# Softmax attention and a linear attention on one Trainium2 core: the end of the last unit rebuilt, and a build-time scheduler given new weights

## The chip, the cores and the metric

The kernel runs on one core of one Trainium2 chip. The metric is the time of one execution on the device in microseconds (us). The kernel before was run five times: 786.75, 781.05, 789.01, 781.58 and 782.21 us, so the median is 782.21 us.

The core has five engines that run side by side, each with its own list of instructions in a fixed order: TensorE (PE, matrix products into PSUM), VectorE (DVE), ScalarE (ACT, activation functions such as Exp), GpSimd (POOL), and SyncE (SP), which issues most DMA transfers. An instruction waits on semaphores for its inputs; all that stands behind it on its engine waits with it.

## The reference

Two independent blocks on sequences of 2048 rows of 512 numbers, 32 heads of 16, in bf16. Their outputs stand side by side in `out[2048, 1024]`.

```python
# A: full softmax attention
q, k, v = split(x @ wqkv)                        # [32, 2048, 16] each
p = softmax(q @ k.T * 16**-0.5)                  # [32, 2048, 2048]
a = merge(p @ v) @ wo
# B: linear attention with a learned feature map
phi = lambda t: concat(softmax(t @ w_phi), softmax(-(t @ w_phi)))   # 16 -> 32 features
kv, z = phi(k).T @ v, phi(k).sum(rows)
b = merge((phi(q) @ kv) / (phi(q) @ z + 1e-6)) @ wo
```

A makes 32 x 2048 x 2048 exponentials, and these are most of the kernel's work.

## The kernel before, in words

**Units and tiles.** A's work is cut into 32 units: a group of four heads (`g`, eight of them) for 512 queries (`c`, four of them). A unit has 16 key tiles of 128 keys. For one key tile and one head TensorE makes a score tile of 128 keys by 512 queries (L696, four heads in four row quarters of the array). The exponential comes in two ways:

- On ScalarE (L900): one Exp over two or three score tiles at once, straight out of PSUM into the ring `pT`. There are 645 Exps of two tiles and 86 of three, which makes 1,548 score tiles or 387 key tiles.
- On VectorE: 125 key tiles. A multiply-add (L957) writes an integer that, read as fp16, is a piecewise linear exponential; three more copies with an added phase (L978) go with scaled values `VJ`, so that four such curves add up to a good one. Five of a unit's 16 key tiles (`DK`) may go this way.

Then p @ v follows (L703, four column quarters of the array), which adds up in one PSUM bank per unit; a column of ones in V yields the row sums. When a unit is done, VectorE copies its bank to `X` (L750), SyncE sends the sums through DRAM so that their reciprocals come back spread over the partitions (`sums`, `scr`, `Yd`), and GpSimd multiplies (L782). After eight units the rows of a query block are projected (L1023), copied to `OA` and stored (L1039).

**B runs beside A.** Its steps are released when A has reached given shares of its key tiles (`b0`, `b1`, `b2`). The key half has 16 steps, and each has 32 small products of 34 columns (L1147).

**The order is planned when the kernel is built.** `_Sched` holds a queue per stream of tasks, each with an estimated duration and latency. It places next the task that can start earliest, moved by the stream's weight in `_W`, and so writes each engine's list. The chip follows that list with semaphores and no clock of its own. How many key tiles go to VectorE is no constant: it falls out of the planned times (`src_a`, `src_d`). `act_exp` plans an Exp of n tiles at 0.187 + 0.3657 n us.

**Fillers.** Before each TensorE task `_fill` looks at the planned activity of the array in the 3.42 us before (`_recent`). If TensorE would be idle anyway, it inserts products of zero (L730, four in a group) while the activity is under `ACTIVE` = 0.60; under `FORCE` = 0.40 it inserts one even where that delays the task. There are 448 of them, from 65 us on.

**The last unit** does without the way through DRAM (`last_unit`). One fp32 product (L799) spreads the row sums over the partitions into a bank of the pool `G`, which has four banks. VectorE takes four reciprocals of 128 columns each (L805), and after each one multiplies (L808). Meanwhile TensorE has added the other units' share of the four output row groups (L815), each in a `G` bank of its own; the last product of a group (L821) needs that part's multiply. Then three row groups are copied by ScalarE (L1031) and one by VectorE (L1035) into `OA`, which has two places, and stored by SyncE. Five range checks of the sums (L838) run on VectorE in between; they set a flag that leads to a slow general path when a sum is out of range.

Of the kernel before, what the change touches and what calls it, by code (L numbers as in the profile page):

```python
# [157 lines left out]
class _Sched:  # L158
# [5 lines left out]
    MM = 0.216  # L164
    PE_LAT = 0.21
    WINDOW = 3.42
    ACTIVE = 0.60
    FORCE = 0.40

    def __init__(self):  # L170
        self.free = {}
        self.busy = {}
        self.streams = {}
        self.end = 0.0
        self.mode = None
        self.rows = [0.0] * 4
        self.port = {"dve": 0.0, "pool": 0.0}
        self.urgent = None
        self.last_port = None
        self.filler = None  # L180
        self.ahead = lambda: 0
        self.active = collections.deque()
        self.nfill = 0
        self.nforce = 0
# [39 lines left out]
    def _choose(self, eng, ss):  # L224
        cand = []
        for s in ss:
            if not s["q"] and s["src"] is not None:
                s["src"](s)
            if s["q"]:
                t = s["q"][0]  # L230
                if t.prep is not None:
                    t.prep(t)
                r = self._ready(t) if t.gate is None or t.gate() else None
                if r is not None:
                    st = self._start(t, r)
                    w = s["w"]
                    cand.append([st, st + (w(t) if callable(w) else w) - _W["age"] * (st - r), s, r])
        if not cand:
            return None
        if eng == "pe" and self.urgent is not None:  # L240
            u = [c for c in cand if c[2] is self.urgent]
            if u:
                due = max(u[0][3], self.free["act"] + self.ahead() - self.MM - self.PE_LAT - _W["early"])
                for c in cand:
                    t = c[2]["q"][0]
                    if t.mode != "r" and c[0] + t.dur + self.SWITCH > due + 0.02:
                        c[1] += _W["guard"]
        c = min(cand, key=lambda c: c[1])
        return c[0], c[2]

    def run(self):
        while True:
            best = None
            for eng, ss in self.streams.items():
                c = self._choose(eng, ss)
                if c is not None and (best is None or c[0] < best[0]):
                    best = c
            if best is None:
                break
            self._place(best[1]["q"].popleft(), best[0])  # L260
        left = {e: [len(s["q"]) for s in ss] for e, ss in self.streams.items()}
        assert not any(any(v) for v in left.values()), left
# [10 lines left out]
    def _fill(self, t, start):  # L273


        e = max(self.free["pe"], max(self.rows))
        back = 0.0 if t.mode == "c" else self.SWITCH
        x = e if self.mode == "c" else e + self.SWITCH
        while True:
            a = self._recent(max(x, start - back))  # L280
            late = x + self.MM + back > start
            if a >= (self.FORCE if late else self.ACTIVE) or not self.filler(x):
                break
            self._record(x, x + self.MM, 1.0)
            x += self.MM
            self.nfill += 1
            self.nforce += late
            self.mode = "c"
            self.rows = [x] * 4
            self.free["pe"] = x  # L290
            if late:
                start = x + back
                break
        return start

    def _place(self, t, start):
# [41 lines left out]
        if t.then is not None:  # L338
            t.then(t)


_W = dict(tp=-0.226, qa=-0.02, qd_r=0.115, qd_o=0.235, pj=-0.051, pa_n=3, pa_w=0.053, pd_n=0, pd_w=0.105,
          b=-0.067, op=-0.004, dx=-0.238, dxe=-0.193, dev=-0.248, dop=-0.322, dn=-0.245, da=-0.165, dad=0.113,
          dek=-0.101, av=-0.057, kf=-0.03, v=0.039, kv=0.004, qf=-0.017, y=-0.203, t=0.061, o=0.176, df=-0.163,
          dred=-0.076, dv=-0.053, dkv=-0.118, dy=-0.02, dd=0.003, dob=-0.124, dmn=0.059, akf=-0.019,
          aqf=-0.072, aot=-0.365, age=0.03, early=0.0, guard=0.346, cut=5, lead=6, b0=0.286, b1=0.54, b2=0.99,
          p0=8, p1=30, p2=6.012, psh=0, pn=1, ps=-0.308, el=2, both=0, va=16, ka=8, ota=0, xlat=3.6)

_LOG2E = 1.4426950408889634
_NPH = 4  # L350
# [5 lines left out]
def _main_path(nc, es, P, dsem, flag, A_x, A_wqkv, A_wo, B_x, B_wqkv, B_w_phi, B_wo, out):  # L356
# [18 lines left out]
    SC = _Sched()  # L375
# [130 lines left out]
    def put(s, t):  # L506
        s["q"].append(t)
        return t
# [73 lines left out]
    def bank_of(f):  # L582
        return PS[:, f.res["b"].idx, :]
# [164 lines left out]
    def make_unit_end(u):  # L748
# [5 lines left out]
        def after_x(_):  # L754
            xi = xv.res["x"].idx
            d1 = put(sp_q, _Task("sp", 0.5, dma(d_s1[u % 2], lambda e, t, i: e.dma_start(
                sums[:, 16 * u:16 * u + 16], X[16 - g % 2:128:32, xi, :])), [xv], lat=2.2,
                rel=[lambda: [xv.res["x"]]]))
            if u == NU - 1:
                col.append(d1)  # L760
# [35 lines left out]
    def last_unit(xv, xi, c):  # L796


        bc = put(pe_op, _Task("pe", 0.9, pe_group(1, lambda e, t, i: e.matmul(  # L799
            PS[:, t.res["b"].idx, :], sel[:], X[:, xi, :], start=True, stop=True)), [xv], lat=PL, pre=[t_sel],  # L800
            need=[("b", G, 1, 4)]))
        parts = []
        for k in range(4):
            cs = slice(128 * k, 128 * k + 128)
            r = put(dv_n, _Task("dve", 0.98, one("dve", lambda e, t, cs=cs: e.reciprocal(  # L805
                Yd[:, parts[0][0].res["y"].idx if parts else t.res["y"].idx, cs], PS[:, bc.res["b"].idx, cs])), [bc], lat=DL,
                need=[] if parts else [("y", y_sl, 1, 4)], rel=[lambda: [bc.res["b"]]]))
            m = put(dv_n, _Task("dve", 0.22, one("dve", lambda e, t, cs=cs: e.tensor_tensor(  # L808
                Oo[:, parts[0][1].res["o"].idx if parts[0][1].res else t.res["o"].idx, cs], X[:, xi, cs],
                Yd[:, parts[0][0].res["y"].idx, cs], ALU.mult)), [r], lat=DL, need=[] if parts else [("o", oo_sl, 1, 1)],  # L810
                rel=[lambda: [parts[0][0].res["y"]]] + ([lambda: [xv.res["x"]]] if k < 2 else [])))
            parts.append((r, m))
        firsts = []
        for st in range(4):
            f = put(pe_op, _Task("pe", 4 * MM, pe_group(4, lambda e, t, p, st=st: e.matmul(  # L815
                bank_of(t), OT[:, c % 2, p, st * 128:(st + 1) * 128], WOp[:, p, :] if p < 3 else WOl[:, 0, :],
                start=(p == 0), stop=False)), [mul[8 * c + p] for p in (1, 3, 5, 6)] + [l_wo] + wol, need=[("b", G, 1, 1)]))
            firsts.append(f)
        for st in range(4):
            f = firsts[st]  # L820
            t = put(pe_op, _Task("pe", MM, pe_group(1, lambda e, t, i, st=st, f=f: e.matmul(  # L821
                bank_of(f), Oo[:, parts[0][1].res["o"].idx, st * 128:(st + 1) * 128], WOl[:, 1, :], start=False, stop=True)),
                [f, parts[st][1]], lat=PL))
            out_rows(c, st, f, t, st % 4 != 3)

    cnt = sb("cnt", [128, 8], F32)
    good = sb("good", [128, 1], BF)
# [65 lines left out]
    def act_exp(qk):  # L893

        pieces, b, n = qk.pieces, qk.first, len(qk.pieces)
        us = 0.187 + 0.3657 * n

        def ex_emit(e, t):
            p = slots(t)[0].idx
# [27 lines left out]
    def dve_kt(u, kt):  # L927
# [7 lines left out]

        def gate():

            if sum(x.left == 0 for x in G) > 1:
                return True
            return not any(s["q"] and s["q"][0].need and s["q"][0].need[0][1] is G  # L940
                           and all(d.done for d in s["q"][0].deps) for s in one_bank)
# [73 lines left out]
    pe_qd["src"] = src_d  # L1015

    d_oa = [dsem("oa0"), dsem("oa1")]
    op_done = {}

    def out_proj(c):  # L1020
        op_done[c] = []
        for st in range(4):
# [1 line left out]
                bank_of(t), OT[:, c % 2, p, st * 128:(st + 1) * 128], WOp[:, p, :], start=(p == 0), stop=(p == 3)),  # L1024
                [mul[8 * c + 2 * p + 1] for p in range(4)] + [l_wo], [("b", G, 1, 1)])
            op_done[c].append(t)
            out_rows(c, st, first, t, False)

    def out_rows(c, st, first, t, on_act):
        if on_act:  # L1030
            ev = put(ac_ev, _Task("act", 0.49, one("act", lambda e, t: e.activation(  # L1031
                OA[:, t.res["o"].idx, :], bank_of(first), ACT.Copy)), [t], lat=AL,
                need=[("o", oa_sl, 1, 1)], rel=[lambda: [first.res["b"]]]))
        else:
            ev = put(dv_op, _Task("dve", 0.61, one("dve", lambda e, t: e.tensor_copy(  # L1035
                OA[:, t.res["o"].idx, :], bank_of(first))), [t], lat=DL,
                need=[("o", oa_sl, 1, 1)], rel=[lambda: [first.res["b"]]]))
        r0 = (4 * c + st) * 128
        put(sp_q, _Task("sp", 0.5, dma(lambda t: d_oa[ev.res["o"].idx], lambda e, t, i: e.dma_start(  # L1039
            out[0][r0:r0 + 128, 0:512], OA[:, ev.res["o"].idx, :])), [ev], lat=2.2, rel=[lambda: [ev.res["o"]]]))  # L1040

    BDr = sb("BDr", [128, 4, 16], BF)
    BD = sb("BD", [128, 4, 128], BF)
# [1235 lines left out]
```

## Time and profile before

| | |
|---|---|
| median of five runs | 782.21 us |
| the profiled execution's own time | 788.49 us |
| its span, first to last instruction | 786.7 us |
| its mean granted TensorE clock | 0.979 |
| busy: ACT, PE, DVE, POOL | 754.6, 742.0, 716.3, 153.4 us |
| last Exp (L900) ends | 771.2 us |
| Exps of two tiles / of three / key tiles on VectorE | 645 / 86 / 125 |

The profiled execution lies at the slow end of the five. "Busy" counts the time in which an engine has an instruction running; neighbouring instructions overlap, so the mean duration of a group is longer than the distance from one start to the next.

### The profile page before, as it was taken

The numbers are of one execution on the slowest core, as the hardware profiler recorded it, in microseconds if no ns is written. First come the engines' busy times: TensorE is split into PE (matmuls) and PEld (weight loads), VectorE is DVE, ScalarE is ACT, GpSimd is POOL, SyncE is SP. The second block draws the span as 40 slices with busy tenths as digits, with TensorE's granted clock in tenths as the row PEclk, the third lists the DMA queues.
The fourth block names the chain that finished last, engine by engine and source line by source line (L and its number), as shares of the span: only waits on it lengthen the run. The fifth ranks groups of instructions, "written<-read, shape, count | busy, mean of one in ns | idle before, by whom it ended". The sixth has DMA issues, their size and how long they took to land.

```text
span 786.7 us, 17442 instructions
## 1 busy us (share of the span) xinstructions
PE 742.0 (94%) x7331; PEld 218.2 (28%) x7331; DVE 716.3 (91%) x1275; ACT 754.6 (96%) x818; POOL 153.4 (19%) x218
## 2 busy tenths in 40 slices
PE   8999999998999999989999999999999999999995
PEld 3322222231222222222222232222232322222221
DVE  2799999997999799898999989999999998999995
ACT  6999999997999899899999999999999999999992
POOL 3320101200112213121312032312212122031210
PEclk9999999997999799799999999999999999999999
DMA  6100000180001000000000000000000010000000
GB/s 156 60 15 15 12 9 19 36 195 19 30 18 30 18 17 15 6 14 20 16 15 18 30 18 28 24 18 16 25 23 25 21 48 17 20 18 30 25 23 30
DMA packets 43872, 23.40 MB, mean 30 GB/s; under 512 B 31180, under 2 KB 39820, under 8 KB 43788
## 3 DMA queue, kind: packets, MB, share of 16 engines
q1 hardware_dynamic: 42204, 21.45, 9.8%
q8 instruction: 58, 0.95, 0.5%
q10 hardware_dynamic: 1584, 0.79, 0.4%
q14 instruction: 26, 0.21, 0.1%
HBM read 11.81 MB, written 4.45 MB: 21 GB/s over the span
## 4 chain that ended last, share of the span: by engine, by line
ACT 84%; PE 10%; DVE 4%; DMA 2%; issue 0%; POOL 0%; SPq 0%; POOLq 0%
ACT pT L900 80%; PE PS L696 3%; PE PS L703 3%; ACT e_k L1117 2%; ACT eT L1180 1%; PE PS L594 1%; DVE rg L957 1%; PE PS L549 1%; DMA sums<-X 1%; DMA Yd<-scr 1%; DVE Wf L1102 1%; DVE rg L978 1%; PE PS L597 0%; PE PS L1114 0%; DVE Yd L805 0%; PE PS L730 0%
## 5 line engine op out<-in xcount | busy, mean ns | idle before, releaser
L900 ACT ACTIVATE pT<-PS 128x1024 bf16<-128x1024 f32 (+1 forms) x731 | 716.6, 1121 | 10.5 <-PE PS L696 10.2
L957 DVE TENSOR_SCALAR rg<-PS 128x512 uint16<-128x512 f32 x500 | 325.1, 683 | 27.6 <-PE PS L696 24.5
L696 PE MATMUL PS<-QT,KT 32*128 32x512 bf16 x2048 | 315.2, 389 | 24.6 <-ACT pT L900 19.6
L978 DVE TENSOR_SCALAR rg<-rg 128x2048 uint16<-128x2048 uint16 x375 | 249.4, 701 | 3.6 <-PE PS L703 3.3
L703 PE MATMUL PS<-pT,VP 128*32 128x512 bf16 x1548 | 155.8, 394 | 6.6 <-ACT pT L900 3.9
L696 PEld LDWEIGHTS PS<-QT,KT 32*128 32x128 bf16 x2048 | 78.8, 91 | 289.0 <-ACT pT L900 217.4
L703 PE MATMUL PS<-rg,VJ 128*32 128x512 f16 x1500 | 139.2, 391 | 1.2 <-DVE rg L978 1.0
L703 PEld LDWEIGHTS PS<-pT,VP 128*32 128x32 bf16 x1548 | 40.2, 94 | 90.9 <-issue 47.3
L1127 POOL TENSOR_TENSOR w<-e_k,stat 128x512 bf16<-128x512 bf16 x32 | 33.3, 1057 | 123.1 <-DVE stat L1123 70.3
L703 PEld LDWEIGHTS PS<-rg,VJ 128*32 128x32 bf16 x1500 | 37.7, 95 | 58.0 <-issue 28.9
L703 PE MATMUL PS<-rg,VP 128*32 128x512 f16 x500 | 50.2, 392 | 0.0
L782 POOL TENSOR_TENSOR OT<-X,Yd 128x256 bf16<-128x256 f32 x30 | 23.3, 796 | 104.1 <-DMA Yd<-scr 67.5
L1217 POOL TENSOR_TENSOR w<-w 128x272 f32<-128x272 f32 x32 | 23.8, 760 | 97.7 <-DVE w L1203 57.9
L782 POOL TENSOR_TENSOR Oo<-X,Yd 128x256 bf16<-128x256 f32 x30 | 22.7, 778 | 96.2 <-DMA Yd<-scr 60.2
L730 PE MATMUL PS<-ones_t,zer 128*32 128x512 bf16 x448 | 41.4, 392 | 0.0
L597 PE MATMUL PS<-xT,w 128*128 128x512 bf16 x124 | 35.4, 383 | 1.4 <-DVE xT L569 0.9
L1227 POOL TENSOR_TENSOR w<-w,den 128x256 bf16<-128x256 f32 x32 | 19.7, 635 | 45.0 <-DVE rg L978 27.0
L1203 DVE TENSOR_TENSOR w<-PS,stat 128x408 f32<-128x408 f32 (+1 forms) x48 | 25.3, 528 | 0.7
L750 DVE COPY X<-PS 128x512 f32<-128x512 f32 x32 | 21.9, 683 | 3.4 <-PE PS L703 3.3
L633 POOL TENSOR_SCALAR KT<-KT,hmask 128x512 bf16<-128x512 bf16 x12 | 8.3, 695 | 77.4 <-DVE KT L607 47.8
L1120 DVE TENSOR_REDUCE stat<-e_k 128x64 f32<-128x1024 bf16 x16 | 19.4, 1216 | 2.2 <-ACT e_k L1117 2.1
L1114 PE MATMUL PS<-Wf,xT 128*128 128x512 bf16 x64 | 20.6, 413 | 0.0
(100 smaller groups left out, 430.2 us busy)
## 6 DMA issues: line engine op xcount, KB each, us to landing
Yd<-scr SPq DMA_DIRECT2D x31, 256.0 KB
out_dram<-OA SPq DMA_DIRECT2D x16, 128.0 KB, 1.7
out_dram<-e_k SPq DMA_DIRECT2D x16, 128.0 KB, 1.7
OT<-Oo SPq DMA_DIRECT2D x60, 16.0 KB, 1.8
w<-in_A_wqkv_dram SPq DMA_DIRECT2D x2, 384.0 KB, 4.2
OT<-in_A_x_dram SPq DMA_DIRECT2D x1, 512.0 KB, 4.7
w<-in_A_wqkv_dram ACTq DMA_DIRECT2D x1, 512.0 KB, 6.3
WOp<-in_A_wo_dram SPq DMA_DIRECT2D x1, 512.0 KB, 6.6
```

Of the source, the lines that this page charges most:

```text
L597: return e.matmul(bank_of(t), w[:, ct, c0:c0 + 128], xT[:, ct, c * 512:(c + 1) * 512], start=(ct == 0), stop=(ct == 3))
L696: return e.matmul(out_ap, KT[32 * r:32 * r + n, g, kt * 128:(kt + 1) * 128], QT[32 * r:32 * r + n, c, g // 2, :], start=True, stop=True, t ...
L703: return e.matmul(PS[32 * r:32 * r + 32, pvb[u].idx, :], lhs(8 * (g // 2) + 2 * r + g % 2), rhs(r), start=t.res["first"], stop=t.res["last ...
L730: P.op("pe", lambda e, r=r: e.matmul(PS[32 * r:32 * r + 32, pvb[u].idx, :], zer[:], ones_t[:].unsqueeze(1).broadcast_to([128, 4, 128]), st ...
L750: xv = _Task("dve", 0.61, one("dve", lambda e, t: e.tensor_copy(X[:, t.res["x"].idx, :], PS[:, pvb[u].idx, :])), [], lat=DL, need=[("x", x ...
L782: ms.append(put(po_n, _Task("pool", 0.7, one("pool", lambda e, t, cs=cs: e.tensor_tensor(OT[:, c % 2, g // 2, cs] if even else Oo[:, ms[0] ...
L900: return e.activation(pT[:, p:p + n, :].rearrange("p a n -> p (a n)"), PS[:, b:b + n, :].rearrange("p a n -> p (a n)"), ACT.Exp, scale=0.25)
L957: return e.tensor_scalar(rg[:, q0.res["i"].idx, 512 * r:512 * r + 512], PS[:, qk.res["D"].idx, :], ya, yb, ALU.mult, ALU.add)
L978: ad = put(dv_ad, _Task("dve", 0.59, one("dve", lambda e, t, j=j: e.tensor_scalar(rg[:, t.res["j"].idx, :], rg[:, q0.res["i"].idx, :], flo ...
L1127: ph.append(put(po_phi, _Task("pool", 1.03, one("pool", lambda e, t, a=a: e.tensor_tensor(pk[ph[0].res["k"].idx][:, 512 * a:512 * a + 512] ...
L1203: muls.append(put(dv_y, _Task("dve", 0.485, one("dve", lambda e, t, yv=yv, lo=lo, n=n: e.tensor_tensor(ysv[r0.res["y"].idx][:, 136 * lo:13 ...
L1217: ad = [put(po_y, _Task("pool", 0.73, one("pool", lambda e, t, k=k: e.tensor_tensor(y3(0)[:, 2 * k:2 * k + 2], y3(0)[:, 2 * k:2 * k + 2], ...
```

## The change

It has four parts.

1. **Last unit.** The fp32 product is made in two halves of 256 columns, which go to the two banks of the pool `A_bank` instead of one `G` bank. Reciprocals 0 and 1 stay on VectorE; 2 and 3 become Ln and then Exp with scale -1 on ScalarE.
2. **Last output rows.** The four row groups go to four places in `rg`, a buffer of the VectorE exponentials that is free by then, instead of the two of `OA`, and each store has its own semaphore.
3. **The scheduler's estimates.** An Exp of n tiles is planned at 0.064 + 0.4265 n us; the transfer of the sums at 2.6 us instead of 2.2. `ACTIVE` becomes `fill` = 0.575 and `FORCE` becomes `force` = 0.41. A score task of the VectorE way is held back when the planned end of VectorE lies more than `dg` = 9 us after that of TensorE; if no task at all can be placed, the gates are lifted once.
4. **New weights** for a dozen streams.

```diff
-    ACTIVE = 0.60
-    FORCE = 0.40
...
-                r = self._ready(t) if t.gate is None or t.gate() else None
+                r = self._ready(t) if t.gate is None or self.lifted or t.gate() else None
...
-            if a >= (self.FORCE if late else self.ACTIVE) or not self.filler(x):
+            if a >= (_W["force"] if late else _W["fill"]) or not self.filler(x):
...
-_W = dict(tp=-0.226, qa=-0.02, qd_r=0.115, qd_o=0.235, pj=-0.051, pa_n=3, pa_w=0.053, pd_n=0, pd_w=0.105,
-          b=-0.067, op=-0.004, dx=-0.238, dxe=-0.193, dev=-0.248, dop=-0.322, dn=-0.245, da=-0.165, dad=0.113,
-          dek=-0.101, av=-0.057, kf=-0.03, v=0.039, kv=0.004, qf=-0.017, y=-0.203, t=0.061, o=0.176, df=-0.163,
-          dred=-0.076, dv=-0.053, dkv=-0.118, dy=-0.02, dd=0.003, dob=-0.124, dmn=0.059, akf=-0.019,
-          aqf=-0.072, aot=-0.365, age=0.03, early=0.0, guard=0.346, cut=5, lead=6, b0=0.286, b1=0.54, b2=0.99,
-          p0=8, p1=30, p2=6.012, psh=0, pn=1, ps=-0.308, el=2, both=0, va=16, ka=8, ota=0, xlat=3.6)
+_W = dict(tp=-0.226, qa=-0.039, qd_r=0.115, qd_o=0.235, pj=-0.051, pa_n=3, pa_w=0.053, pd_n=0, pd_w=0.104,
+          b=-0.067, op=-0.004, dx=-0.205, dxe=-0.193, dev=-0.248, dop=-0.359, dn=-0.214, da=-0.165, dad=0.113,
+          dek=-0.081, av=-0.051, kf=-0.03, v=0.039, kv=0.004, qf=-0.012, y=-0.203, t=0.061, o=0.243, df=-0.163,
+          dred=-0.076, dv=-0.053, dkv=-0.118, dy=-0.02, dd=0.003, dob=-0.078, dmn=0.041, akf=-0.019,
+          aqf=-0.089, aot=-0.317, age=0.03, early=0.0, guard=0.346, cut=5, lead=6, b0=0.286, b1=0.54, b2=0.99,
+          p0=8, p1=30, p2=6.012, psh=0, pn=1, ps=-0.308, el=2, both=0, va=16, ka=8, ota=0, dm=0.4, force=0.41,
+          fill=0.575, dg=9.0)
...
-                sums[:, 16 * u:16 * u + 16], X[16 - g % 2:128:32, xi, :])), [xv], lat=2.2,
+                sums[:, 16 * u:16 * u + 16], X[16 - g % 2:128:32, xi, :])), [xv], lat=2.2 + _W["dm"],
...
-        bc = put(pe_op, _Task("pe", 0.9, pe_group(1, lambda e, t, i: e.matmul(
-            PS[:, t.res["b"].idx, :], sel[:], X[:, xi, :], start=True, stop=True)), [xv], lat=PL, pre=[t_sel],
-            need=[("b", G, 1, 4)]))
+        bcs = [put(pe_op, _Task("pe", 0.45, pe_group(1, lambda e, t, i, k=k: e.matmul(
+            PS[:, t.res["b"].idx, 256 * k:256 * k + 256], sel[:], X[:, xi, 256 * k:256 * k + 256], start=True, stop=True)),
+            [xv], lat=PL, pre=[t_sel], need=[("b", A_bank, 1, 2)])) for k in range(2)]
...
+            if k < 2:
+                r = put(dv_n, _Task("dve", 0.98, one("dve", lambda e, t, cs=cs, y_at=y_at, bc=bc: e.reciprocal(
+                    y_at(t), PS[:, bc.res["b"].idx, cs])), [bc], lat=DL,
+                    need=[] if parts else [("y", y_sl, 1, 4)], rel=[lambda bc=bc: [bc.res["b"]]]))
+            else:
+                ln = put(ac_ev, _Task("act", 0.29, one("act", lambda e, t, cs=cs, y_at=y_at, bc=bc: e.activation(
+                    y_at(t), PS[:, bc.res["b"].idx, cs], ACT.Ln)), [bc, parts[0][0]], lat=AL, rel=[lambda bc=bc: [bc.res["b"]]]))
+                r = put(ac_ev, _Task("act", 0.29, one("act", lambda e, t, y_at=y_at: e.activation(
+                    y_at(t), y_at(t), ACT.Exp, scale=-1.0)), [ln], lat=AL))
...
-            out_rows(c, st, f, t, st % 4 != 3)
+            out_rows(c, st, f, t, True)
...
-        us = 0.187 + 0.3657 * n
+        us = 0.064 + 0.4265 * n
...
+            if SC.free["dve"] > SC.free["pe"] + _W["dg"]:
+                return False
...
+        def dst(t):
+            return rg[:, st, 0:512].bitcast(BF) if last else OA[:, t.res["o"].idx, :]
+        need = [] if last else [("o", oa_sl, 1, 1)]
+        if last and st < 3:
             ev = put(ac_ev, _Task("act", 0.49, one("act", lambda e, t: e.activation(
-                OA[:, t.res["o"].idx, :], bank_of(first), ACT.Copy)), [t], lat=AL,
-                need=[("o", oa_sl, 1, 1)], rel=[lambda: [first.res["b"]]]))
+                dst(t), bank_of(first), ACT.Copy)), [t], lat=AL, need=need, rel=[lambda: [first.res["b"]]]))
```

## The prediction

> **What bounds the kernel now.** I read the page's slices first, then ScalarE's waits, the windows around the low places, and the timeline and waits of the last 16 us.
>
> ```profile
> DVE  2799999997999799898999989999999998999995
> ACT  6999999997999899899999999999999999999992
> PEclk9999999997999799799999999999999999999999
> ...
> L900 ACT ACTIVATE pT<-PS 128x1024 bf16<-128x1024 f32 (+1 forms) x731 | 716.6, 1121 | 10.5 <-PE PS L696 10.2
> ```
>
> ScalarE is full from 7 us (first data) to 771.2 us (last Exp). All that it lost on the way is 10.2 us of waiting for scores (L696). The row of the clock has three low slices, and finer windows say that both are one thing:
>
> ```profile
> 176.00:180.00 4.00, 2.73 (x34) 0.78 (x29) 2.89 (x6) 3.62 (x4) 0.00 (x0) 1.00 0.17 42
> 180.00:190.00 10.00, 10.00 (x70) 1.82 (x69) 7.09 (x12) 6.94 (x7) 1.45 (x2) 0.50 0.08 28
> 252.00:255.00 3.00, 2.42 (x45) 0.91 (x44) 3.00 (x7) 3.00 (x4) 1.50 (x3) 1.00 0.05 8
> 255.00:265.00 10.00, 9.66 (x72) 1.97 (x68) 6.11 (x11) 7.79 (x9) 3.26 (x4) 0.50 0.08 28
> 320.00:323.00 3.00, 2.33 (x51) 1.01 (x51) 2.90 (x7) 3.00 (x4) 1.83 (x2) 1.00 0.00 0
> ```
>
> Columns: stretch, its length, busy us of PE, PE weight loads, DVE, ACT, POOL, then the granted clock. Three times TensorE is little used for some 3 us, and then it runs at half clock for about 10 us, at 180, 255 and 323 us. ScalarE's waits in 175-200, 250-270 and 320-340 us are 4.0, 2.2 and 3.6 us: 9.8 of the 10.2. One such dip costs 3.3 us. The profiled execution took 788.49 us (span 786.7 and 1.8 around it); without dips it would be 788.49 - 9.8 = 778.7. The runs' median of 782.21 is 3.5 above that, about one dip; I take it as one, and 789.01 as three. So ScalarE's list bounds the kernel up to 771 us, and after that the end does:
>
> ```profile
> 773.73 0.95 DVE L805 RECIPROCAL Yd<-PS 128x128 f32<-128x128 f32 x1
> ...
> 778.32 0.33 PEld L815 LDWEIGHTS PS<-WOp,OT 128*128 128x128 bf16 x3 [2.66 <-DVE Yd L805]
> 778.33 0.82 PE L815 MATMUL PS<-WOp,OT 128*128 128x512 bf16 x3 [2.17 <-DVE Yd L805]
> ...
> 779.62 1.09 ACT L1031 ACTIVATE OA<-PS 128x512 bf16<-128x512 f32 x2 [8.42 <-PE PS L821]
> 780.24 4.04 SPq L1039 DMA_DIRECT2D out_dram<-OA  x4
> ...
> 782.06 0.60 ACT L1031 ACTIVATE OA<-PS 128x512 bf16<-128x512 f32 x1 [1.35 <-DMA out_dram<-OA]
> 782.46 0.69 DVE L1035 CAST OA<-PS 128x512 bf16<-128x512 f32 x1 [1.76 <-DMA out_dram<-OA]
> ```
>
> Two waits show. The fourth row group (L815) waits for the last reciprocal, since the spread sums hold one of the four G banks. The third and fourth copies wait until a store of `OA` has landed. The last store is issued at 783.2 (its issue took 1.10 us, the others 0.33), and the span ends 3.5 us later.
>
> **The end, step by step** (trace clock; X is copied by 772.39).
> - *Sums spread.* L799 held TensorE for 0.96 us (772.45 to L815's 773.41). Two halves are 0.48 each: the first result at about 773.1, L815 again from 773.41. Both `A_bank` banks are free, since the last Exp ended at 771.2.
> - *Row groups.* Groups of L815 start 0.865 apart (773.41, 774.27, 775.14). With all four G banks free the fourth starts at 776.00 and ends at 776.87. L821 starts there instead of at 779.20: **2.3 us** gained, if the multiplies are ready.
> - *Reciprocals.* VectorE's first check ends at 773.14; reciprocal 0 takes 0.95, the multiply 0.21 to the next start. So R0 773.16, M0 774.15, R1 774.36, M1 775.35. ScalarE starts after R0, because the `Yd` place is R0's, at 774.15. Ln and Exp of 128 columns appear nowhere in the trace; bounds are 0.27 us, the distance between two Copies of 128 columns (L647), and 0.37, their duration. I take 0.37, as each waits for the one before: both parts done at 775.65. M2 and M3 end by 776.1, or 776.8 if the second check (0.7 us) comes in between. The last L821 starts at 777.52, so the whole chain is covered; were it one microsecond longer, it would show. Behind M2 and M3 on VectorE stand only checks and the last copy; behind the Lns on ScalarE the three row copies, which TensorE releases later anyhow.
> - *A table switch?* The Trainium skill, "ScalarE: Activation LUTs", "What ACT_TABLE_LOAD costs", prices a change of function set at 1.28 us and a drain of 1.38, which would speak against Ln. But its section on table sets puts Exp and Ln in one set, and that is the set the program preloads: the trace's one load (1.28 us at 0.79) is followed by none. I add nothing; with one load before the first Ln, the parts would be done near 778.3 and about 1.1 us of the gain gone.
> - *Copies and stores.* Copies on ScalarE start 0.42 us after their L821: 777.29, 777.78, 778.28, ending at 778.87 (0.49 apart, 0.60 long). VectorE's ends near 778.6. Nothing waits for a landing. SyncE has nothing else in its queue (the sums' issue ended at 772.97); four issues of 0.33 end with one at about 779.25 instead of 783.2.
>
> Sum: **-3.9 us**; -3.0 if VectorE's copy is put after the checks and the last issue is slow as before, -4.5 if the long issue goes too. About 2.3 is the bank, 1.5 the spare places; the split alone does not set the end, but without it M3 would come at 778.6 and take back half a microsecond.
>
> **Planned Exp times.** Start to start, a two-tile Exp takes 0.919 us in the trace (mean of 627) and a three-tile one 1.336 (81). The old plan said 0.918 and 1.284, the new says 0.917 and 1.344. The work costs the same, but the planner now sees 86 x 0.060 = 5.2 us more on ScalarE. One key tile costs ScalarE 4 x 0.459 = 1.84 us, and VectorE 4 x 0.63 + 3 x 0.62 = 4.4. To be level again it moves 5.2 / (1.84 + 4.4) = 0.8 tiles. VectorE has about 30 us idle between 40 and 770 us outside the dips, room for six tiles. I take one tile: **-1.8 us**. The new weights can do the same either way; their row is nowhere in a trace. Bounds: three tiles more (-5.5), two fewer (+3.7), nearest to zero and one.
>
> **The rest of the plan.** The sums' later planned landing: once (at 177 us) VectorE waited 1.1 us for it, because it took 5.0 us behind B's loads; 0.4 does not cover that. Gain between 0 and 0.4 us of VectorE, taken as 0. The 9 us gate: each task is placed at the earliest start, so an engine's planned end runs a task ahead, not 9 us; taken as never acting, 0. Lifted gates act only when nothing can start: 0.
>
> **Fillers against dips.** 448 fillers are 112 groups of 0.216 us, 24 us of TensorE; a lower `fill` removes some. That gains nothing, since ScalarE waited just 0.4 us outside dips. What can it cost? I weighed each product of the trace by its columns (0.42 ns each, from 0.216 us per 512) and by its share of the array, in windows of 3.413 us laid so that one begins at 180.0; the other dips begin 22 and 20 windows later, and each lasts three. The windows just before the dips hold 0.305, 0.353 and 0.346 of full activity; the lowest others at full clock, between 6 and 777 us, hold 0.400, 0.414 and 0.416. The limit lies between. Two of three dips come after L1147 products, whose real activity is far below the planned 0.4. The Trainium skill, "TensorE: Matmul & The Clock Gate", part 1, has the same window, free-running, but its rule asks only for no idle gap over about 3 us. Here TensorE's longest wait was 1.1 us before the first dip and under 0.4 before the other two: by the rule no dip at all and a free change, by the trace dips from low activity at 3.3 us each. The trace decides. `fill` down 0.025 and `force` up 0.01 act against each other; I take 0, with bounds of two dips more and one fewer (+6.6, -3.3).
>
> **Sum.** On the profiled execution 788.5 - 3.9 - 1.8 = 782.8 with its three dips; with one, as in the median run, 782.2 - 5.7 = **776.5**.
>
> **The rivals.**
> - *The plan gains more* (chance 0.28): three key tiles move, or one and a dip fewer: 782.2 - 3.9 - 5.2 = 773.1. For it: VectorE's 30 us; against: L978 and L957 already run at over 95% outside dips.
> - *The end's gain is eaten* (0.21): a tile fewer on VectorE or one dip more, 776.5 + 3.5 = 780. For it: 16 key steps of B, each able to dip.
> - *Slower* (0.08 slower at all, 0.04 by over 1%): the lower `fill` takes windows of B's key half below the limit. Place: 250 to 450 us; price 3.3 each. From 5.7 / 3.3, that is two more dips than before, the gain is gone; with three more, 786.4.
> - *The change doesn't do what it says*: the split reciprocals don't set the end, and the 9 us gate never acts. The time stays 776.5 then too; it is in the forecast (0.43).
>
> **How the numbers follow.** 776.5 has 0.43, with its own range 774 to 779. The others are 773.1, 780 and 786. Leaving a tenth at each end gives 771.5 to 782. A measurement of this kernel tells about 1% from no change, that is 774.4 to 790.0: faster 0.33 (the second case and a little of the first), slower 0.04, within 0.63.
>
> **What would show it.** L821's first start 5.7 us after the last Exp's end instead of 8.0; no L815 wait for `Yd`; copies with no wait for a store; the span's end about 11.6 us after the last Exp instead of 15.5; one table load; 126 key tiles on VectorE (504 L957); as many low clock slices as before or one more. It would be wrong if the last Exp's end moved by more than 4 us with the clock equal, or if dips came in numbers.

## The result and the profile after

The changed kernel took 778.43 us (median of 42 executions), the kernel before 785.47 on the same chips (79 executions): a ratio of 0.9917, with a 95% interval of 0.9899 to 0.9936. That is 0.83% faster, or 6.5 us of 785.47. (Ratios, here and below, leave out slow executions, those more than 1.5% above the fastest of the same kernel, while medians and means are of all; so a ratio is not the quotient of the medians.) The five runs that the prediction started from had a median of 782.21; the longer series puts the kernel before higher. The profiled execution of the changed kernel took 776.69 us, with a span of 775.0 and a mean clock of 0.993.

From the page of the changed kernel, the slices and the groups of Exps and of the VectorE way (in a group: count, busy us, mean ns, idle time before it):

```profile
DVE  2799999999999999988799889999999999999996
ACT  6999999999999999999999989999999999999995
PEclk9999999999999999998999999999999999999999
...
L913 ACT ACTIVATE pT<-PS 128x1024 bf16<-128x1024 f32 (+1 forms) x746 | 714.9, 1112 | 5.2 <-PE PS L700 5.0
L973 DVE TENSOR_SCALAR rg<-PS 128x512 uint16<-128x512 f32 x504 | 326.4, 682 | 20.8 <-PE PS L700 18.4
```

ScalarE's waiting for scores has fallen from 10.2 to 5.0 us, and there are 504 first steps of the VectorE way, which is 126 key tiles. What is not on this page is in the groups by shape: 692 Exps of two tiles and only 53 of three (before 645 and 86), and one of a single tile.

Two stretches at half clock are left, seen in windows around them (columns as in the prediction: stretch, its length, busy us of PE, PE weight loads, DVE, ACT and POOL with the number of instructions, granted clock, DMA share, GB/s):

```profile
355.00:362.00 7.00, 6.35 (x90) 2.18 (x90) 7.00 (x13) 7.00 (x10) 1.45 (x3) 1.00 0.05 12
362.00:369.00 7.00, 6.86 (x41) 1.30 (x41) 4.76 (x8) 5.34 (x6) 1.49 (x2) 0.54 0.00 0
454.00:458.00 4.00, 2.52 (x27) 0.60 (x28) 4.00 (x10) 2.82 (x4) 1.23 (x2) 1.00 0.09 28
458.00:461.00 3.00, 3.00 (x27) 0.72 (x26) 1.94 (x4) 1.93 (x2) 2.71 (x5) 0.52 0.16 59
```

The clock records give them 6.8 and 3.4 us, two windows and one: a dip need not last three.

The end, from the timeline; the last Exp ends at 764.02:

```profile
766.01 0.96 DVE L813 RECIPROCAL Yd<-PS 128x128 f32<-128x128 f32 x1
...
767.06 0.28 ACT L817 ACTIVATE Yd<-PS 128x128 f32<-128x128 f32 x1 [3.04 <-DVE Yd L813]
...
767.37 0.31 ACT L819 ACTIVATE Yd<-Yd 128x128 f32<-128x128 f32 x1
767.58 0.26 ACT L817 ACTIVATE Yd<-PS 128x128 f32<-128x128 f32 x1
...
768.83 0.81 PE L828 MATMUL PS<-WOp,OT 128*128 128x512 bf16 x3
...
769.69 1.03 PE L834 MATMUL PS<-WOl,Oo 128*128 128x512 bf16 x4
...
770.11 1.57 ACT L1052 ACTIVATE rg<-PS 128x512 bf16<-128x512 f32 x3 [1.93 <-PE PS L834]
770.73 1.82 SPq L1058 DMA_DIRECT2D out_dram<-rg  x4
```

The fourth row group (L828 at 768.83) waits for nobody, and the three ScalarE copies run without a break, so both old waits are gone. The last product (L834, L821 before) starts 5.67 us after the last Exp instead of 8.0, and the last store is issued 8.08 us after it instead of 11.98. From the last Exp to the end it is 10.93 us instead of 15.46.

So the difference of these two profiled executions, 11.7 us, has two parts: 4.5 at the end, and 7.2 by which the last Exp ends earlier. The second holds the dips (30.7 us at half clock before, 10.2 after) and whatever the new plan is worth.

### The profile page after: what moved, and what is told of

The parts are those of the page before. It is cut to its first block, busy times and chain, and to the rows that moved or that the text cites. A ratio compares the mean times of both kernels' runs of the same rounds, so it can differ in the third digit from the quotient of the medians.

```text
span 775.0 us, 17444 instructions
## 1 busy us (share of the span) xinstructions
PE 734.7 (95%) x7321; PEld 218.5 (28%) x7321; DVE 712.6 (92%) x1280; ACT 753.5 (97%) x837; POOL 153.1 (20%) x218
## 4 chain that ended last, share of the span: by engine, by line
ACT 81%; PE 9%; DVE 5%; DMA 3%; POOL 1%; issue 0%; SPq 0%; ACTq 0%
ACT pT L913 77%; PE PS L707 3%; PE PS L700 3%; DVE rg L973 2%; DVE rg L994 2%; ACT e_k L1136 2%; DMA sums<-X 1%; ACT eT L1199 1%; DMA scr<-rin 1%; DMA Yd<-scr 1%; DMA OT<-in_A_x_dram 1%; PE PS L828 0%; PE PS L1195 0%; ACT KT L629 0%; ACT VP L609 0%; PE PS L598 0%
## 5 line engine op out<-in xcount | busy, mean ns | idle before, releaser
L734 PE MATMUL PS<-ones_t,zer 128*32 128x512 bf16 x424 | 38.2, 384 | 0.0
```

The lines of the kernel that those rows point to most:

```text
L734: P.op("pe", lambda e, r=r: e.matmul(PS[32 * r:32 * r + 32, pvb[u].idx, :], zer[:], ones_t[:].unsqueeze(1).broadcast_to([128, 4, 128]), st ...
```

## The experiments

To separate these I used the timed executions. Each lists its span and mean clock. The half-clock stretches in the clock records are 3.413 us long or a multiple of it (but for the last, which the end of the record cuts), so I count in windows of 3.413 us: an execution has (1 - clock) x span / 1.707 of them. One straight line for each kernel, with a slope common to all, through 274 executions (all but the single ones of e10 to e12 and the 11 of the kernel before beside e9), span = floor + slope x windows, gives 1.28 us per window and leaves 1.07 us of scatter. A kernel's floor is its span with no window at half clock, as its line gives it. The ends in the first column are from one profiled execution each.

| kernel | last Exp to end, profile | floor (+- two errors) | half-clock windows, mean (+- error) |
|---|---|---|---|
| before | 15.46 | 775.7 +- 0.4 | 7.5 +- 0.3 |
| changed | 10.93 | 771.6 +- 0.4 | 4.9 +- 0.5 |
| e1 end only | 12.25 | 773.1 +- 0.6 | 7.1 +- 0.6 |
| e2 plan only | 16.20 | 776.2 +- 0.7 | 7.3 +- 0.7 |
| e3 Exp times only | 16.86 | 781.4 +- 0.5 | 5.4 +- 0.5 |
| e4 fillers by small products | 10.95 | 784.3 +- 0.7 | 7.3 +- 1.1 |
| e6 old thresholds | 10.93 | 771.9 +- 0.6 | 3.5 +- 0.5 |
| e7 old Exp times | 13.46 | 776.0 +- 0.6 | 3.2 +- 0.5 |
| e8 old weights | 10.95 | 772.7 +- 0.6 | 6.5 +- 0.9 |
| e9 more idle fillers | 10.93 | 770.7 +- 0.9 | 3.0 +- 0.4 |

Three reserves. The runs came from several chips, and windows may differ between chips (the changed kernel: 4.3 +- 0.5 in the result, 6.6 +- 1.0 beside e6 to e8). The count takes in half clock behind the last Exp, where TensorE runs out of work: 0.7 of a window in the trace of the kernel before, 2.4 in e2's, none in that of the changed kernel; what such a window costs is not separated. And with a slope of its own for each kernel (before 1.38 +- 0.08, changed 1.23 +- 0.08) the floors are 774.9 and 771.8, so the 4.1 us between them could be 3.1.

**e1: the end alone**, on the kernel before.

```diff
+ last_unit and out_rows of the changed kernel, d_ol
  (weights, thresholds and planned times of before)
```

> The kernel before with the new last unit and the new last output rows only; estimates and weights as before, so every engine's list is that of before up to the last unit. Theory (the end's gain is its own): last Exp's end to the span's end 11.0 us instead of 15.5, so 4.5 us faster at the same clock, ratio 0.994; the clock dips as often as before. Rival (the gain sits in the new plan, and the end is hidden or eaten by stores landing): ratio 1.000, within 0.1%.

Ratio 0.9939 (0.991 to 0.9967); floor 2.6 us lower. The gain is real and the end's own. But the profile has 12.25 us from the last Exp to the end, not 11.0. The steps are those of the changed kernel to the hundredth (L830 starts 5.67 after the last Exp). From the issues of `out_dram`, the stores of e1:

```profile
L1051 SPq DMA_DIRECT2D out_dram<-rg x4: 332/346/444, 776.6 to 778.0; - x4
...
DMA to landing us min/median/max: 1.7/1.7/3.3
```

and of the changed kernel:

```profile
L1058 SPq DMA_DIRECT2D out_dram<-rg x4: 332/341/452, 770.7 to 772.1; - x4
...
DMA to landing us min/median/max: 1.7/1.7/1.8
```

The last store lands 1.5 us late. A store tells of its landing by sixteen notices (updates of its semaphore). Of this one's, fifteen are there by 779.84 and the last comes at 781.32; SyncE's list of final waits stops at just this semaphore, from 779.97 to 781.34. The last packet of the store ends at 779.84, behind an 8 KB packet of code (an instruction queue, q14) that ended at 779.83, and a 16 KB packet of code (queue q8) runs from 780.11 to 781.21. So SyncE waited for a notice that came after the code; that the code held it up is likely by the times, and not shown. In the changed kernel the 16 KB packet starts as soon after the last Exp (10.17 us, e1 10.20), but there the last notice was in before it (773.92, 9.90 us after the last Exp).

**e2: the plan alone.**

```diff
- last_unit and out_rows of the changed kernel
+ last_unit and out_rows of the kernel before
```

> The changed kernel with the last unit and the last rows of before: new estimates, fillers and weights only. 126 key tiles go to VectorE and 53 Exps have three tiles. Theory: the span at full clock falls by about 0.9 us (one tile fewer on ScalarE, 33 fewer triple Exps against it), and fewer dips give about 1.5 more in the median: ratio 0.997. Rival 1 (the plan is the gain): ratio 0.992. Rival 2 (the plan gains nothing, all is the end): 1.000.

Ratio 1.000 (0.9971 to 1.003); floor 0.5 us higher, of which 0.7 is a longer issue of the last store (1.75 us where the kernel before has 1.10). Rival 2 holds within the interval: no gain of the plan at full clock is seen. Floor less the end puts the last Exp at 760.0 in e2 and at 760.2 before (760.7 in the changed kernel), each good to about half a microsecond. The tile is there, and so are the fewer triples. By the median distances of the trace (0.904 us for two tiles, 1.331 for three) the Exps need 697.6 us before and 696.6 after, 1.0 less and not 1.8, and that 1.0 lies within what the fit can tell.

**e3: the planned Exp times alone**, on the kernel before.

```diff
-        us = 0.187 + 0.3657 * n
+        us = 0.064 + 0.4265 * n
```

> The kernel before with only the planned Exp time changed to 0.064 + 0.4265 n. The build places 123 key tiles on VectorE, two fewer than before, 676 Exps of two tiles and 68 of three. My step in the prediction said one tile more for this edit. By the price of a tile (1.84 us each) the span at full clock is 3.7 us longer, plus 0.7 for 18 fewer triples: ratio 1.005. Rival (a plan with true times makes up for it by fewer waits): 1.000 or less.

```profile
L957 DVE TENSOR_SCALAR rg<-PS 128x512 uint16<-128x512 f32 x492 | 318.3, 682 | 23.3 <-PE PS L696 20.7
```

The page's group shows the 492 steps, 123 tiles. The floor rises by 5.7 us to 781.4; the ratio is only 1.0016 (0.999 to 1.0042), as it had two half-clock windows fewer. The tile's price holds here (4.3 us of it is the last Exp, 764.5 against 760.2; 3.7 + 0.7 were expected). My reason for the tile doesn't: told that ScalarE has more to do, the planner gave VectorE less.

**e4: fillers where B's small products are overrated.**

```diff
-  lat=PL if part == 3 else 0.0, mode="c", area=0.4,
+  lat=PL if part == 3 else 0.0, mode="c", area=0.1,
```

> The changed kernel with one number more: the planned activity of B's small products (34 columns) is 0.1 instead of 0.4, near what their columns come to, so that the planner puts fillers there (544 instead of 424 zero products, 125 key tiles on VectorE, 59 triples). Theory (dips come from windows whose real activity is below 0.36, and the planner overrates these products): mean clock 0.997 or more in most runs, half the dips or fewer, median 2 to 3 us below the changed kernel. Rival (the dips have another cause, or the fillers cost as much as they save): as many dips as the changed kernel, ratio to before 0.992 to 0.995.

Ratio 1.0104 (1.0067 to 1.0141): slower than before. The profiled execution had one window at half clock, and yet:

```profile
L913 ACT ACTIVATE pT<-PS 128x1024 bf16<-128x1024 f32 (+2 forms) x745 | 719.4, 1108 | 11.4 <-PE PS L700 10.5
```

ScalarE waits for scores twice as long as in the changed kernel, without dips to blame. The theory misses on both counts: there were 7.3 windows on average, and the floor is 12.7 us above the changed kernel's. The whole plan had shifted (another order, 125 tiles, 30 groups of fillers more), so the run doesn't say whether forced fillers or the new order cost the time.

**e5: the changed kernel again**, beside e6 to e8 on one chip.

> The changed kernel itself, on the chip of the three kernels that follow, so that they can be set against it. From the parts done alone (the end 0.994, the plan 1.000) the product is 0.994; the result said 0.992. If the parts add up, 0.994 and a last Exp's end within 1 us of that of the plan done alone at equal clock; if the two parts help each other (a rival), 0.990 or less.

Ratio 0.9963 (0.9928 to 0.9999), medians of 781.04 us against 785.38. It had 6.6 windows, and the kernel before 6.7 on that chip. With equal windows the medians lie 4.3 us apart and the means 3.4, near the floor's 4.1, with nothing from dips. In the result the windows were 4.3. The kernel before has no clock on record there; 6.5 windows are worked back from its mean time, which gives 2.2 x 1.28 = 2.8 us beside the floor's 4.1. That this adds up to the 6.9 us between the means is so by construction. It is an estimate; that the two ratios differ by the number of dips fits it, and their intervals overlap.

The profiled execution of e5 has 34 us at half clock before the last Exp, and ScalarE waits for scores longer than in the kernel before:

```profile
L913 ACT ACTIVATE pT<-PS 128x1024 bf16<-128x1024 f32 (+1 forms) x746 | 716.5, 1112 | 12.6 <-PE PS L700 12.1
```

So the fall from 10.2 to 5.0 us in the result's profile goes with that execution's dips and is no sign of a better plan.

**e6: thresholds of before.**

```diff
-  force=0.41, fill=0.575
+  force=0.40, fill=0.60
```

> The changed kernel with the filler thresholds of before (0.60 and 0.40). The build keeps 126 key tiles on VectorE, 59 triples instead of 53, 444 zero products instead of 424. Theory (the two thresholds act against each other, my 0 in the prediction): as many half-clock windows per run as the changed kernel (4 on the earlier chip, within 1.5), ratio to before within 0.2% of it. Rival (the lower voluntary threshold costs dips): two half-clock windows fewer here and 2 to 3 us faster.

Ratio 0.9935 (0.9908 to 0.9962), same floor, three windows fewer than e5 on the same chip (3.5 +- 0.5 against 6.6 +- 1.0). This favours the rival: the new thresholds cost dips. But the edit changes the order on ScalarE and VectorE too, and the intervals of the two ratios overlap.

**e7: old planned Exp times in the changed kernel.**

```diff
-        us = 0.064 + 0.4265 * n
+        us = 0.187 + 0.3657 * n
```

> The changed kernel with the old planned Exp time (0.187 + 0.3657 n). The build places 123 key tiles on VectorE instead of 126, and 88 triples instead of 53. By the price of a tile 3 x 1.84 = 5.5 us more for ScalarE, less 1.4 for 35 triples: 4 us slower than the changed kernel, ratio to before about 0.999. Rival (tiles don't matter as VectorE's list has room elsewhere; only dips do): within 1 us of the changed kernel at equal clock.

Ratio 0.9977 (0.9948 to 1.0006), floor 4.4 us above the changed kernel. The page shows the 123 tiles:

```profile
L973 DVE TENSOR_SCALAR rg<-PS 128x512 uint16<-128x512 f32 x492 | 319.3, 682 | 26.1 <-PE PS L700 23.9
```

The size was expected, but 2.5 of it is the end: SyncE is done at 776.58, and the program then waits until TensorE reaches its last step at 778.99. A branch on TensorE took 4.16 us there and 0.39 in the changed kernel; a packet of code (8 KB) ends in it, at 778.50. Only 1.8 is the earlier work, where the three tiles lost, with 35 more triples against them, should have cost 4: here the price of a tile is not borne out. So the edit that loses two tiles in the kernel before (e3) keeps three in this one: its effect depends on the other weights.

**e8: weights of before.**

```diff
- the changed stream weights
+ the stream weights of before (dm, force, fill, dg kept)
```

> The changed kernel with the stream weights of before, new estimates and thresholds kept. 125 key tiles on VectorE, 76 triples. Theory (the weights are worth a tile, less the triples): 0.9 us slower than the changed kernel, ratio to before 0.995. Rival (the weights were fitted to the new estimates and the waits between engines come back without them): 4 us or more slower, ratio 0.999 or above.

Ratio 0.9984 (0.9953 to 1.0016), floor 1.1 us above the changed kernel, as the theory had it for the tile; the ratio is above the 0.995 expected, with as many windows as e5.

**e9: more voluntary fillers.**

```diff
-  fill=0.575
+  fill=0.70
```

> The changed kernel with the voluntary threshold 0.70 instead of 0.575 and nothing else. All engines keep their lists in the same order; TensorE gets 508 zero products instead of 424, only where the plan has it idle. Theory (the dips hang on the activity of single windows, and more voluntary fillers lift it): fewer half-clock windows per run than the changed kernel, by 1.5 or more, at 1.3 us each 2 us faster; ratio to before 0.991 or less, the floor at full clock unchanged. Rival (idle filling doesn't reach the windows that dip, which lie where TensorE is late): the same number of windows, ratio as the changed kernel's (0.992 and 0.996 so far).

Ratio 0.9859 (0.9814 to 0.9904), 776.04 us against 787.65; 3.0 windows, and 7.5 for the kernel before on that chip; the floor stays within its error. The clean edit of the study: it adds 84 zero products to TensorE's list where the plan leaves it idle, and in the traces the order of all else is that of the changed kernel, on every engine. The theory holds, with the reserve of six executions and no run of the changed kernel on that chip. It has the lowest ratio of the study, though its interval still touches the result's. The slices of its profiled execution show one dip left (6.8 us at 183.8), after the stretch in which B's inputs are loaded:

```profile
ACT  6999999997999999999999999999999999999995
PEclk9999999998999999999999999999999999999999
```

**e10, e11, e12: the end in pieces**, one profile each, on the kernel before.

```diff
  e10: end of e1, but  if k < 2  ->  if k < 4    (all reciprocals on VectorE)
  e11: e10 with the rows through OA as before
  e12: kernel before with the rows through rg
```

> The kernel before with the spread sums in A_bank and the spare places, but all four reciprocals on VectorE. From the last Exp's end to the span's end 15.46 us before, 10.93 in the changed kernel. My step said that the split is worth half a microsecond here: 11.5 us. Rival (the reciprocals were the bound): 13 us or more. A fetch of code at the end can add 1.1 to 1.5 us to either.

> The kernel before with the spread sums in the two A banks only; four reciprocals on VectorE, the last rows through the two places of OA. My step: the first L821 starts 5.7 us after the last Exp's end instead of 8.0, and the end follows by as much: 13.1 us from the last Exp to the end. Rival (the two places of OA or the last reciprocal take the gain back): 14.5 us or more.

> The kernel before with the four spare places only; the spread sums stay in their G bank and the reciprocals on VectorE. My step: no copy waits for a store, 1.5 us gained: 13.9 us from the last Exp to the end, the first L821 still at 8.0. Rival (the stores then queue behind each other): 15 us or more.

From the last Exp to the end: 11.90, 12.81 and 15.28 us (before 15.46; all three parts 12.25 in e1 and 10.93 in the changed kernel). The copies in the timeline of e11:

```profile
775.63 1.09 ACT L1040 ACTIVATE OA<-PS 128x512 bf16<-128x512 f32 x2 [6.09 <-PE PS L830]
778.08 0.60 ACT L1040 ACTIVATE OA<-PS 128x512 bf16<-128x512 f32 x1 [1.36 <-DMA out_dram<-OA]
```

and of e12:

```profile
780.11 1.57 ACT L1036 ACTIVATE rg<-PS 128x512 bf16<-128x512 f32 x3 [8.42 <-PE PS L821]
```

e11 has the bank's gain (6.09 us of waiting instead of 8.42) and still waits for a store; its 12.81 is near the 13.1 expected. e12 has its copies in one go as expected. The starts of the last store's issue, counted from the last Exp, divide the end without what comes after it: 11.98 before, 10.09 with the bank (e11), 8.48 with bank and spare places (e10), 8.08 with the split as well (e1 and changed), and 10.41 with the spare places alone (e12). So by the last issue the bank is worth 1.9, the places 1.6 either way, the split 0.4.

What comes after that issue changes two of these. e10 ends 1.0 us behind the changed kernel, not 0.4, because of VectorE's range checks. With two more reciprocals on VectorE the flag that they set comes 9.5 us after the last Exp instead of 8.1 (e10, then the changed kernel):

```profile
779.62 0.15 DVE L855 TENSOR_SCALAR flag<-PS 1x1 int32<-1x1 f32 x1 [0.26 <-PE PS L853]
...
771.96 0.15 DVE L859 TENSOR_SCALAR flag<-PS 1x1 int32<-1x1 f32 x1 [0.26 <-PE PS L857]
```

SyncE loads the flag after its last issue, in the changed kernel 0.06 us after it, in e10 0.75: it waits for the checks. At the end the split is thus worth 1.0 us. e12 ends hardly before the kernel before, at the rival's number (15 or more) but not by its cause: the first three stores land after 2.0 to 2.4 us, only the last is late. The landings of e12:

```profile
L1042 SPq DMA_DIRECT2D out_dram<-rg x4: 332/343/448, 780.7 to 782.1; - x4
...
DMA to landing us min/median/max: 2.0/2.3/4.0
```

In the packet records a 16 KB code packet runs from 783.23 to 784.98, and the last packets of the stores start only after it, up to 785.61. SyncE's wait for the last store costs 2.0 us; without it e12 would end near 13.3 us (13.9 expected).

## Why the prediction was right, step by step

The forecast was 776.5 against a baseline of 782.2, so 5.7 us; the measured change is 6.5 us of 785.47, and 778.43 lies in the range.

- *What bounds the kernel*: held. ScalarE's list up to the last Exp, then the end.
- *The end, -3.9 with -4.5 as its bound*: 4.53 in the profiles, 2.6 +- 0.7 in the floors of e1, where the last notice came late. The step times came out as worked: L834 5.67 us after the last Exp (5.67 forecast), the last issue 8.08 (8.05). Ln and Exp took 0.28 and 0.31 us, 1.12 for the chain of four against 1.5 taken, and no table load was seen. The 0.6 beyond the forecast is the last store's issue, 0.45 us long instead of 1.10; the forecast named that length without a cause. In the three traces where the issue is long, a packet of code runs in it.
- *How the end divides*: by the last issue, the bank 1.9 us (2.3 forecast), the spare places 1.6 (1.5), the split 0.4 (0.5). At the end the split is worth 1.0: the forecast let the range checks trail at no cost, and without the split they set the end.
- *The tile, -1.8*: one tile came, as forecast, but for a reason that fell. e3 shows the edit alone losing two tiles; how many tiles VectorE gets is set by edit and weights together. And I left the triples at 86: 33 fewer took back about 0.8. At full clock the plan alone is worth 0.2 +- 0.8 us (the last Exp of e2 against that of before). That is the term of the sum that was mis-sized.
- *The dips, 0*: at 3.3 us a dip of three windows. The price is 3.8 by the slope. A score that comes a little late may delay an Exp inside the overlap with the one before it, with no wait booked; that would explain the rest, and is not shown. Their number fell by 2.2 windows in the result, as estimated, and by 0.2 in e5. So some 2.8 us of the result's 6.9 (of means) are fewer dips that I had put at nothing; they made up for the tile. That the total came so near is in this part luck: with dips as in e5 the gain is 3 to 4 us. Whether the new plan itself makes dips rarer stays open: plan and end have 7.3 and 7.1 windows alone, the same chip's kernel before 8.1.
- *Thresholds act against each other*: e9 shows, with its reserve, that voluntary fillers do lower the dips, so the lower `fill` was probably a loss, and e6 points the same way.
- *The 9 us gate*: with it set out of reach the build gives the same program. It never acts.
- *The activity limit*: weighed as in the prediction, dips in the changed kernel follow windows with 0.335 and 0.365 of full activity, and one of 0.353 passes. So the limit is near 0.36, blurred by matmul records that a trace lacks. The same weighing of all fourteen traces (windows between 6 and 757 us) bears it out: all 31 dips follow windows of 0.23 to 0.38; of some 2,980 full-clock windows that another such window follows, one is below 0.345 (0.32 in e5, whose trace lacks 75 products).

## What to carry to other kernels

Work the end of a kernel out on the trace's own clock, bank by bank and place by place: those starts came true to a few hundredths of a microsecond, while guesses of what a planner will do with a new estimate came true by chance. Follow the sum past the last store too: checks, notices and fetches of code moved the end by 0.6 to 2.5 us here. When one kernel's runs scatter by 2%, set span against mean clock before comparing; the scatter here was a count of half-clock windows at 1.28 us each. Put zero products where TensorE is idle anyway, and see that they move nothing else.

## What the runs showed of the hardware that was not expected

- *Fetches of code fall together with delays at the end.* A 16 KB packet of the instruction queue q8 takes 0.9 to 1.75 us, and over the last 70 us of the changed kernel one comes every 12 to 16 us. Where it runs into the last store's issue, that issue takes 1.10 to 1.75 us instead of 0.33 to 0.45 (before, e2, e3). Where it runs before the last notice is in, the notice comes 0.1 us after the packet ends, and SyncE stops for 1.4 us (e1). Where it runs beside the stores, their last packets come after it (e12). In the changed kernel it starts 0.3 us after the last notice, which makes the 1.3 us between the ends of e1 and the changed kernel. All this is read from times that coincide. What sets the packet's place was not tried, nor was it shifted on purpose.
- *A dip may last one to four windows*: 3.4, 6.8, 10.2 or (e1, e10, e11) 13.7 us in the clock records. It lasts about as long as the activity stays under the same limit: weighed as above, in all fourteen traces, the 39 half-clock windows that another follows hold 0.27 to 0.38, and of the 31 that end a dip 28 hold 0.378 to 0.50 (the others 0.31 to 0.37). So the array need not stand still to be slowed: in the windows before the changed kernel's two dips TensorE's longest gap was 0.37 and 1.08 us.
